# A fused attention and two-MoE kernel on one core: the rational function's square in PSUM, output sums in two banks, shifted tile addresses and a narrow block in half banks

## The chip, the core and the metric

The kernel runs on one core of one Trainium2 chip. Its engines work side by side, each through a queue of its own in a fixed order: TensorE (PE in the rows) multiplies matrices into PSUM, VectorE (DVE), ScalarE (ACT) and GpSimd (POOL) work on whole tiles, SyncE (SP) issues the transfers. PSUM has eight banks here, `ps0` to `ps7`, each 128 partitions by 512 float32; GpSimd is never given a PSUM operand in this kernel. The metric is the device time in microseconds (us), lower is better.

## What is computed

Linear attention (softmax of q over its features, of k over the sequence) feeds a gated MoE, whose output feeds a second MoE with a rational function of its hidden values. The inputs are float32; tokens are 2304, the model width 512, the hidden widths 1536 and 2048.

```python
kv  = einsum('bhsd,bhse->bhde', k_s, v)
x   = einsum('bhsd,bhde->bhse', q_s, kv)      # to (2304, 512)
x   = ((x @ w_a) * (x @ w_b)) @ w_out         # first MoE, d_ff 1536
h   = x @ w_in                                # second MoE, d_ff 2048
P   = a[0] + a[1]*h + a[2]*h**2 + a[3]*h**3
Q   = 1.0 + abs(b[0])*abs(h) + abs(b[1])*h**2
out = (P / (Q + 1e-6)) @ w_out2
```

## The kernel before

Every float32 operand of a product is split into a high and a low part, and a product is three matmuls: high by high, high by low, low by high (`mm3`, lines 444 to 447, and the same in `mult`, lines 598 to 600). The transposed activations lie in `XH` and `XL`, the running sums in `ACC`, weights and split hidden values in cuts of one long tile `wa`, everything unsplit in cuts of `fa`. Tokens are worked in four blocks of 512 and one narrow block of 256.

**First MoE.** `step1` takes one hidden block f of 128 and one token block n: products a and b (`proj`) into two banks, a copy of a by ScalarE (L473), the product by VectorE (L476), the split by ScalarE and VectorE (L479, L480), and then (`rest`) four products with `w_out` into the four banks `Y` = ps0 to ps3, which after three hidden blocks are added to `ACC` by VectorE (`add_acc`, L463). The last group of steps ends with the narrow block.

**Second MoE.** The multiplication by `w_in` goes in 16 slots of a Strassen-Winograd scheme. `operands` makes the sums and differences of the activation blocks (L520 to L527), once for blocks 0 and 1 and once for blocks 2 and 3. A slot makes seven products of six matmuls each (L598 to L600): A11 into `BA`, copied by ScalarE to `BB` (L619); S1 into `BE`, copied to s5; A12 onto `BA`; S2 onto `BB`, added with s5 by VectorE into `BC` (L624); S3 onto `BB`, added with s5 into the SBUF tile h4 (L626); S4 onto `BC`; A22 onto `BB`. The four banks are the same in every slot: BA, BE, BB, BC = 4, 5, 6, 7. The first eight slots also multiply the narrow block, into BE. Each result h goes through `value` (72 times): ScalarE makes |h| and two linear terms (L552 to L554), GpSimd w = w|h| (L559), VectorE the cubic (L558 or, for h4, GpSimd's L556; then L560), ScalarE the reciprocal square root of Q and its square u into SBUF (L562, L563), VectorE the cubic's last step times u (L564), one Newton step of the reciprocal (L566) and the product (L568). `whole` splits the value (ScalarE's L580, GpSimd's L581), and `jobs` multiplies four values by `w_out2` into the banks ps0 to ps3, four hidden blocks for each sum, then adds to `ACC` (L463) and sends the last sum out.

**What sets the order.** All work is first entered in `Plan` with an engine, an estimated duration, a rank and what it reads and writes. `Plan.run` then goes through time by these estimates: of what is ready, it takes the earliest possible start, then the lower rank. The engines' queues are the result. The estimates know nothing of VectorE and GpSimd slowing each other in `value`: only `port=True` work excludes each other there, and `value`'s VectorE work is entered without it. `LATE` is what the second half of `value` adds to its rank, `SOON` what the adds and copies inside a slot take off it.

Of the kernel before, what the change touches and what calls it, by code (L numbers as in the profile page):

```python
# [16 lines left out]
P = 128  # L17
# [97 lines left out]
def tile_kernel(ctx: ExitStack, tc: tile.TileContext, q, k, kx, v, w_a, w_b, w_out, w_in, w_out2, ca, cb, out):  # L115
# [7 lines left out]
    W = 512  # L123
# [13 lines left out]
    LATE, SOON = 1.0, -2.0  # L137
# [43 lines left out]
    fa = Area(o_x + 3 * W, F32, "fa")  # L181

# [284 lines left out]
    def step1(f, n, banks, start, stop, first, final, rank):  # L467
        t0, nb = blocks[n]
        ba, bb = banks
        proj("a", f, n, ba, rank)  # L470
        g, kg = r_g.take()
        g = g[:, :nb]
        act(nb, rank, lambda: nc.scalar.activation(g, ps[ba][:, :nb], AF.Copy), [psk(ba)], [kg])  # L473
        proj("b", f, n, bb, rank)
        p, kp = ps[bb][:, :nb], psk(bb)
        dve(nb, rank, lambda: nc.vector.tensor_tensor(out=p, in0=p, in1=g, op=ALU.mult), [kp, kg], [kp])  # L476
        hl, kh = r_hl.take()
        hh, ll = hl[:, 0, :nb], hl[:, 1, :nb]
        act(nb, rank, lambda: nc.scalar.activation(hh, p, AF.Copy), [kp], [kh])  # L479
        dve(nb, rank, lambda: nc.vector.tensor_tensor(out=ll, in0=p, in1=hh.bitcast(F32), op=ALU.subtract),  # L480
            [kp, kh], [kh])

        def rest():
            w, kw = wtile["o", f]
            for m in range(NCC):
                sl = slice(m * P, (m + 1) * P)
                pe(3, nb, rank, lambda m=m, sl=sl: mm3(ps[Y[m]][:, :nb], w[:, 0, sl], w[:, 1, sl], hh, ll, start, stop),
                   [kw, kh], [psk(Y[m])], fixed=13)
            if not stop:
                return  # L490
            for m in range(NCC):
                o = NCC * t0 + m * nb
                add_acc(o, nb, Y[m], first, rank)
                if final and nb < W:
                    a, xh, xl = ACC[:, o:o + nb], XH[:, m, t0:t0 + nb], XL[:, m, t0:t0 + nb]
                    act(nb, rank, lambda a=a, xh=xh: nc.scalar.activation(xh, a, AF.Copy),
                        [("accr", o)], xk("XH", m, t0, nb))
                    pool(nb, rank, lambda a=a, xh=xh, xl=xl: nc.gpsimd.tensor_tensor(
                        out=xl, in0=a, in1=xh.bitcast(F32), op=ALU.subtract),
                        [("accr", o)] + xk("XH", m, t0, nb), xk("XL", m, t0, nb))  # L500
        return rest

# [6 lines left out]
    def operands(pair, spots, rank, swift):  # L509
# [20 lines left out]
        for r in range(2):  # L530
# [16 lines left out]
    def value(h, kh, ring, rank, inside):  # L547

        V, A, G = nc.vector, nc.scalar, nc.gpsimd
        (u, ku), (w, kw), (z, kz) = r_t.take(), r_t.take(), ring.take()  # L550
        n = W
        act(n, rank, lambda: A.activation(u, h, AF.Abs), [kh], [ku])  # L552
        act(n, rank, lambda: A.activation(z, h, AF.Identity, scale=coef[:, 3:4], bias=coef[:, 2:3]), [kh], [kz], ptr=2)
        act(n, rank, lambda: A.activation(w, u, AF.Identity, scale=bmag[:, 1:2], bias=bmag[:, 0:1]), [ku], [kw], ptr=2)  # L554
# [7 lines left out]
        act(n, rank + LATE, lambda: A.activation(u, w, AF.Abs_reciprocal_sqrt, bias=qbias), [kw], [ku], ptr=1)  # L562
# [40 lines left out]
    BA, BE, BB, BC = 4, 5, 6, 7  # L603
    NAMES = ("A11", "S1", "A12", "S2", "S3", "S4", "A22", "A21")

    def slot(js, j, spots, extra):
# [48 lines left out]
    def jobs(n, g, base, each, banks=Y, by_m=0.0):  # L655

        t0, nb = blocks[n]
        made = {}
        for i, m in [(i, m) for i in range(G2) for m in range(nb // P)]:
            f = g * G2 + i  # L660
            w2, kw2 = w2tile[f]
            sl = slice(m * P, (m + 1) * P)
            rank = step2_rank(base, i * each + m * by_m)
            if m == 0:
                made[i] = whole(f, n, rank - 1.0)
            hl, khl = made[i]
            pe(3, W, rank, lambda m=m, sl=sl, hl=hl, w2=w2, i=i: mm3(
                ps[banks[m]], hl[:, 0, sl], hl[:, 1, sl], w2[:, 0, :], w2[:, 1, :], i == 0, i == G2 - 1),
                [kw2, khl], [psk(banks[m])], fixed=13)
        for m in range(nb // P):  # L670
            r0 = t0 + m * P
# [38 lines left out]
    for s, (n, f, a, b) in enumerate(steps):  # L710
        banks = AB if n == NB - 1 or s < NB * G1 or s % 2 == 0 else AT
# [15 lines left out]
    r_op = Ring(wa.cuts([(9 * 2 + i) * W for i in range(2)] + [i * W for i in range(6)], OP))  # L727
    r_w2 = Ring(wa.cuts([(3 + i) * 2 * W for i in range(5)], 2 * W))
    ha = pair(wa.cuts([8 * 2 * W] + [(NW + i) * 2 * W for i in range(NHL)], 2 * W))
    for i, x in enumerate((XH, XL)):  # L730
        ha.append((x[:, 2:4, 3 * W:4 * W], place(1, 3, 0)[i][1] + place(1, 3, 1)[i][1]))
# [5 lines left out]
    halves = {}  # L737
    w2tile, tile2 = {}, {}
# [82 lines left out]
```

## Time and profile before

| what | value |
|---|---|
| median of 3 runs | 968.3 us (966.86 to 969.74) |
| the profiled execution | 967.09 us, its span 965.3 us |
| TensorE busy | 919.0 us, 95% of the span |
| VectorE busy | 718.2 us, 74% |
| ScalarE busy | 554.9 us, 57% |
| GpSimd busy | 472.7 us, 49% |
| mean granted clock of TensorE | 0.988 |
| DMA queue of SyncE | 130.4 MB, 42.1% of 16 engines |

Read it with care in two places. A matmul is shown longer than the distance to the next one, since matmuls overlap, so TensorE's busy share hides part of its waiting; the distance from start to start is the better measure. And the shares are means over two halves with different work: attention and the first MoE until about 510 us, the second MoE from there. The rest of the 967.09 us beside the span lies around it.

### The profile page before, as it was taken

The page shows a single profiled execution, that of the slowest core. Times are in us where ns is not written, and L with a number is a line of the kernel's source. Part 1 is how long each engine was busy: PE and PEld are TensorE (multiplying, and loading weights), DVE is VectorE, ACT ScalarE, POOL GpSimd, SP SyncE. Part 2 cuts the span into 40 slices and gives each one's busy share as a digit, 9 for nine tenths or more (in the row PEclk, how much of TensorE's full clock was granted, in tenths as well). Part 3 has the DMA queues.
Part 4 walks back from the last instruction along what each step waited for, and adds up shares of the span by engine and source line. Part 5 has one row for each costly group of instructions (what it writes and reads, how often), then busy time and mean ns, then how long its engine had stood idle before and what let it go on. Part 6 is the DMA issues. An engine that isn't in the chain of part 4 may idle for free.

```text
span 965.3 us, 13178 instructions
## 1 busy us (share of the span) xinstructions
PE 919.0 (95%) x4576; PEld 740.9 (77%) x4576; DVE 718.2 (74%) x1035; ACT 554.9 (57%) x1046; POOL 472.7 (49%) x385
## 2 busy tenths in 40 slices
PE   8999999999999999999999879889898899999997
PEld 7677779888888888888778657778786677877775
DVE  5899641465677666766953698888997999879895
ACT  5878552453443444444421777686777667886670
POOL 4554310345423455353620447665768657574652
PEclk9999999999999999999999999999999999999999
DMA  7555510426654566545413432433324255435212
GB/s 257 189 193 152 159 29 1 130 95 222 230 174 131 176 208 213 189 133 174 152 44 96 166 89 86 139 89 106 127 80 160 77 169 179 145 97 164 69 63 87
DMA packets 60034, 131.23 MB, mean 136 GB/s; under 512 B 6464, under 2 KB 14656, under 8 KB 59968
## 3 DMA queue, kind: packets, MB, share of 16 engines
q1 hardware_dynamic: 59680, 130.39, 42.1%
q8 instruction: 36, 0.59, 0.3%
q14 instruction: 30, 0.25, 0.1%
q10 hardware_dynamic: 288, 0.00, 0.0%
HBM read 100.49 MB, written 29.88 MB: 135 GB/s over the span
## 4 chain that ended last, share of the span: by engine, by line
PE 63%; DVE 24%; issue 6%; ACT 4%; POOL 3%; DMA 1%; POOLq 0%; ACTq 0%; DVEq 0%
PE ps L445 18%; PE ps L447 17%; PE ps L446 17%; DVE fa L566 4%; DVE fa L564 4%; DVE fa L568 4%; DVE fa L560 3%; DVE ACC L463 2%; PE ps L598 2%; PE ps L600 2%; PE ps L599 2%; PE ps L426 2%; DVE fa L558 2%; DVE ACC L527 1%; PE ps L400 1%
## 5 line engine op out<-in xcount | busy, mean ns | idle before, releaser
L445 PE MATMUL ps<-XH,wa 128*128 128x512 f32 (+1 forms) x544 | 200.8, 369 | 1.1 <-ACT fa L473 1.1
L447 PE MATMUL ps<-XH,wa 128*128 128x512 f32 (+1 forms) x544 | 196.0, 360 | 0.3 <-POOL wa L288 0.3
L446 PE MATMUL ps<-XL,wa 128*128 128x512 f32 (+1 forms) x544 | 195.9, 360 | 0.0
L445 PE MATMUL ps<-wa 128*128 128x512 f32 (+1 forms) x432 | 168.2, 389 | 5.9 <-DVE ACC L463 3.8
L446 PE MATMUL ps<-wa 128*128 128x512 f32 (+1 forms) x432 | 166.2, 385 | 1.4 <-DVE wa L480 1.4
L447 PE MATMUL ps<-wa 128*128 128x512 f32 (+1 forms) x432 | 165.5, 383 | 0.1
L559 POOL TENSOR_TENSOR fa<-fa 128x512 f32<-128x512 f32 x72 | 108.0, 1511 | 38.4 <-ACT fa L554 31.9
L288 POOL TENSOR_TENSOR wa<-fa,wa 128x512 fp32r<-128x512 f32 x36 | 50.9, 1419 | 141.0 <-ACT wa L287 136.5
L445 PEld LDWEIGHTS ps<-XH,wa 128*128 128x128 f32 x544 | 102.1, 188 | 19.7 <-ACT fa L473 2.2
L447 PEld LDWEIGHTS ps<-XH,wa 128*128 128x128 f32 x544 | 102.2, 188 | 18.3 <-POOL wa L288 0.7
L598 PE MATMUL ps<-XH,wa 128*128 128x512 f32 x224 | 92.4, 413 | 24.8 <-DVE ps L624 11.2
L446 PEld LDWEIGHTS ps<-XL,wa 128*128 128x128 f32 x544 | 102.1, 188 | 16.5
L305 POOL TENSOR_TENSOR fa<-fa 128x256 fp32r<-128x256 f32 x96 | 76.9, 824 | 69.6 <-ACT fa L304 66.7
L476 DVE TENSOR_TENSOR ps<-ps,fa 128x512 f32<-128x512 f32 (+1 forms) x60 | 38.7, 645 | 95.9 <-PE ps L447 95.8
L581 POOL TENSOR_TENSOR wa<-fa,wa 128x512 fp32r<-128x512 f32 x48 | 80.1, 1680 | 53.4 <-ACT wa L580 35.0
L445 PEld LDWEIGHTS ps<-wa 128*128 128x128 f32 x432 | 82.2, 190 | 25.5 <-DVE ACC L463 5.1
L446 PEld LDWEIGHTS ps<-wa 128*128 128x128 f32 x432 | 82.3, 191 | 18.5 <-DVE wa L480 2.9
L479 ACT ACTIVATE wa<-ps 128x512 fp32r<-128x512 f32 (+1 forms) x60 | 33.2, 554 | 109.6 <-DVE ps L476 109.6
L447 PEld LDWEIGHTS ps<-wa 128*128 128x128 f32 x432 | 82.3, 191 | 16.9 <-POOL wa L581 0.9
L599 PE MATMUL ps<-XL,wa 128*128 128x512 f32 x224 | 90.5, 404 | 0.0
L600 PE MATMUL ps<-XH,wa 128*128 128x512 f32 x224 | 90.4, 403 | 0.0
L463 DVE TENSOR_TENSOR ACC<-ps,ACC 128x512 f32<-128x512 f32 (+1 forms) x114 | 71.6, 659 | 22.8 <-PE ps L447 22.7
(108 smaller groups left out, 1822.8 us busy)
## 6 DMA issues: line engine op xcount, KB each, us to landing
wa<-wi SPq DMA_DIRECT2D x120, 256.0 KB, 2.9
wi<-fa SPq DMA_DIRECT2D x64, 256.0 KB, 3.7
wa<-wo SPq DMA_DIRECT2D x32, 512.0 KB, 3.4
fa<-in_moe_w_out SPq DMA_DIRECT2D x28, 512.0 KB, 4.3
fa<-in_moe_w_in SPq DMA_DIRECT2D x16, 512.0 KB, 3.8
wo<-fa SPq DMA_DIRECT2D x32, 256.0 KB, 4.3
fa<-in_moe_w_a SPq DMA_DIRECT2D x12, 512.0 KB, 4.5
fa<-in_moe_w_b SPq DMA_DIRECT2D x12, 512.0 KB, 3.6
```

What stands on the lines that cost most here:

```text
L288: pool(W, rank, lambda: nc.gpsimd.tensor_tensor(out=t[:, 1, :], in0=hf, in1=t[:, 0, :].bitcast(F32), op=ALU.subtract), [kr, kw], [kw])
L305: pool(HALF, rank, lambda: nc.gpsimd.tensor_tensor(out=lo, in0=src, in1=hi.bitcast(F32), op=ALU.subtract), [ksrc, kt], [kt])
L445: nc.tensor.matmul(o, lh, rh, start=start, stop=False)
L446: nc.tensor.matmul(o, lh, rl, start=False, stop=False)
L447: nc.tensor.matmul(o, ll, rh, start=False, stop=stop)
L463: dve(n, rank, lambda: nc.vector.tensor_tensor(out=a, in0=ps[bank][:, :n], in1=a, op=ALU.add), [psk(bank), ("accr", o)], [("accr", o)])
L476: dve(nb, rank, lambda: nc.vector.tensor_tensor(out=p, in0=p, in1=g, op=ALU.mult), [kp, kg], [kp])
L559: pool(n, rank, lambda: G.tensor_tensor(out=w, in0=w, in1=u, op=ALU.mult), [ku, kw], [kw])
L581: pool(W, rank, lambda: nc.gpsimd.tensor_tensor(out=hl[:, 1, :], in0=z, in1=hl[:, 0, :].bitcast(F32), op=ALU.subtract), [kz, kh], [kh])
L598: T.matmul(ps[bank], wh, xh, start=first, stop=False, skip_group_check=True)
L599: T.matmul(ps[bank], wh, xl, start=False, stop=False, skip_group_check=True)
L600: T.matmul(ps[bank], wl, xh, start=False, stop=last, skip_group_check=True)
```

## The change

Five things change; the arithmetic of the result does not, apart from the order of some subtractions in `operands`.

- `value` takes a PSUM bank for every h. The square of the reciprocal square root goes back into that bank (h) instead of an SBUF tile (u), so the three closing VectorE operations each read h from PSUM, and the Newton step writes it. S3's add goes into the bank of S1 instead of the SBUF tile h4, and its first multiplication from GpSimd to VectorE. `LATE` is 0.25 instead of 1.0.
- The four fixed product banks become two rings of three: 5, 3, 4 for BA, BE and the narrow products, 6, 7, 2 for BB and BC. One matmul at the start of the second MoE writes bank 2 once. The output sums have ps0 and ps1 only: `jobs` runs through the four hidden blocks for two token chunks, then for the next two.
- `small`, `mx` and `ks` (320 bytes of each partition, every tile rounded up to 32) are allocated behind `wa` and `fa` instead of in front of them, so `wa` and `fa` begin 320 bytes lower.
- The last group of the narrow block in the first MoE leaves `step1` for `last_narrow`: products a and b share one bank in halves, the output sums two banks in halves, and the ranks are `LAST` = 60.3 and up, so its work falls among the first slots.
- Tiles for operands, `w_out2` and split values take other places in `wa`, and four operand tiles lie in XH and XL where two split values lay.

```diff
-    LATE, SOON = 1.0, -2.0
+    LAST = 60.3
+    LATE, SOON = 0.25, -2.0
...
+
+    small = tiles(2, [P, 4 * C5], F32, "small")
+    mxs = tiles(2, [P, 1], F32, "mx")
+    kss = tiles(2, [P, 1], F32, "ks")
...
+    def last_narrow(fs, ranks):
+        n = NB - 1
+        t0, nb = blocks[n]
+        bank, (y0, y1) = 4, (0, 1)
+        left, right = ps[bank][:, :nb], ps[bank][:, nb:2 * nb]
+        hs = []
+        for f, rank in zip(fs, ranks):
+            for kind, o, ko in (("a", left, ("half", 0)), ("b", right, ("half", 1))):
+                w, kw = wtile[kind, f]
...
+                if kind == "a":
+                    g, kg = r_g.take()
+                    g = g[:, :nb]
+                    act(nb, rank, lambda g=g: nc.scalar.activation(g, left, AF.Copy), [("half", 0)], [kg])
+            dve(nb, rank, lambda g=g: nc.vector.tensor_tensor(out=right, in0=right, in1=g, op=ALU.mult),
+                [("half", 1), kg], [("half", 1)])
...
+        for m in range(NCC):
+            sl = slice(m * P, (m + 1) * P)
+            bank = (y0, y1)[m // 2]
+            y, ky = ps[bank][:, m % 2 * nb:(m % 2 + 1) * nb], ("halfy", m)
...
-        if inside:
-            pool(n, rank, lambda: G.tensor_tensor(out=z, in0=z, in1=h, op=ALU.mult), [kz, kh], [kz])
-        else:
-            dve(n, rank, lambda: V.tensor_tensor(out=z, in0=z, in1=h, op=ALU.mult), [kz, kh], [kz])
         pool(n, rank, lambda: G.tensor_tensor(out=w, in0=w, in1=u, op=ALU.mult), [ku, kw], [kw])
+        dve(n, rank, lambda: V.tensor_tensor(out=z, in0=z, in1=h, op=ALU.mult), [kz, kh], [kz])
...
-        act(n, rank + LATE, lambda: A.activation(u, u, AF.Square), [ku], [ku])
-        dve(n, rank + LATE, lambda: V.scalar_tensor_tensor(
-            out=z, in0=z, scalar=coef[:, 0:1], in1=u, op0=ALU.add, op1=ALU.mult), [kz, ku], [kz], ptr=1)
-        dve(n, rank + LATE, lambda: V.scalar_tensor_tensor(
-            out=u, in0=w, scalar=qbias, in1=u, op0=ALU.add, op1=ALU.mult), [kw, ku], [ku], ptr=1)
-        dve(n, rank + LATE, lambda: V.scalar_tensor_tensor(
-            out=z, in0=u, scalar=2.0, in1=z, op0=ALU.subtract, op1=ALU.mult, reverse0=True), [ku, kz], [kz])
+        rank += LATE
+        act(n, rank, lambda: A.activation(u, w, AF.Abs_reciprocal_sqrt, bias=qbias), [kw], [ku], ptr=1)
+        act(n, rank, lambda: A.activation(h, u, AF.Square), [ku], [kh])
+        dve(n, rank, lambda: V.scalar_tensor_tensor(
+            out=z, in0=z, scalar=coef[:, 0:1], in1=h, op0=ALU.add, op1=ALU.mult), [kz, kh], [kz], ptr=1)
+        dve(n, rank, lambda: V.scalar_tensor_tensor(
+            out=h, in0=w, scalar=qbias, in1=h, op0=ALU.add, op1=ALU.mult), [kw, kh], [kh], ptr=1)
+        dve(n, rank, lambda: V.scalar_tensor_tensor(
+            out=z, in0=h, scalar=2.0, in1=z, op0=ALU.subtract, op1=ALU.mult, reverse0=True), [kh, kz], [kz])
...
-    BA, BE, BB, BC = 4, 5, 6, 7
...
+        ba, be, bb, bc = r_free.take(), r_free.take(), r_seed.take(), r_seed.take()
...
-        dve(W, R(0.2) + SOON, lambda: V.tensor_tensor(out=h4, in0=ps[BB], in1=s5, op=ALU.add), [psk(BB), k5], [k4])
+        dve(W, R(0.2) + SOON, lambda: V.tensor_tensor(out=ps[be], in0=ps[bb], in1=s5, op=ALU.add), [psk(bb), k5], [psk(be)])
...
-    def jobs(n, g, base, each, banks=Y, by_m=0.0):
+    def jobs(n, g, base, each, banks=None, by_m=0.5):
...
+        banks = banks or Y2 * 2
...
+                rank = step2_rank(base, i * each + m // 2 * by_m + m * 0.01)
...
+    spare = [(x[:, 2 + r, 3 * W:4 * W], place(1, 3, r)[i][1]) for i, x in enumerate((XH, XL)) for r in range(2)]
+    r_op = Ring(wa.cuts([(6 * 2 + i) * W for i in range(2)], OP) + spare + wa.cuts([(7 * 2 + i) * W for i in range(2)], OP))
+    r_w2 = Ring(wt(9, 0, 1, 3, 4))
+    ha = pair(wt(8, NW, NW + 1, NW + 2, 2, 5))
...
+    r_free, r_seed = Ring((5, 3, 4)), Ring((6, 7, 2))
+    Y2 = (0, 1)
```

The order of the queues up to about 480 us is the same in both. Two places of the second MoE show what moved. The number after an underscore is a tile's running number; in the changed kernel `ps`, `wa` and `fa` have lower ones. L603, L605 and L607 are there what L564, L566 and L568 are before, L597 and L598 what L558 and L560 are, L663 and L465 what L624 and L463 are.

VectorE's queue ahead of the add that makes `BC` in the seventh slot, in the kernel before:

```order
L568 SCALAR_TENSOR_TENSOR fa_89<-fa_89 128x512
L566 SCALAR_TENSOR_TENSOR fa_89<-fa_89,qbias_66 128x512
L564 SCALAR_TENSOR_TENSOR fa_89<-fa_89,coef_64 128x512
L568 SCALAR_TENSOR_TENSOR fa_89<-fa_89 128x512
L566 SCALAR_TENSOR_TENSOR fa_89<-fa_89,qbias_66 128x512
L564 SCALAR_TENSOR_TENSOR fa_89<-fa_89,coef_64 128x512
L568 SCALAR_TENSOR_TENSOR fa_89<-fa_89 128x512
L566 SCALAR_TENSOR_TENSOR fa_89<-fa_89,qbias_66 128x512
L568 SCALAR_TENSOR_TENSOR fa_89<-fa_89 128x512
L624 TENSOR_TENSOR ps7_87<-ps6_86,fa_89 128x512
```

VectorE's queue ahead of the same slot's add in the changed kernel:

```order
L603 SCALAR_TENSOR_TENSOR fa_83<-fa_83,coef_64,ps7_81 128x512
L465 TENSOR_TENSOR ACC_73<-ps0_74,ACC_73 128x512
L605 SCALAR_TENSOR_TENSOR ps7_81<-fa_83,qbias_66,ps7_81 128x512
L465 TENSOR_TENSOR ACC_73<-ps1_75,ACC_73 128x512
L607 SCALAR_TENSOR_TENSOR fa_83<-ps7_81,fa_83 128x512
L597 TENSOR_TENSOR fa_83<-fa_83,ps4_78 128x512
L597 TENSOR_TENSOR fa_83<-fa_83,ps5_79 128x512
L598 SCALAR_TENSOR_TENSOR fa_83<-fa_83,coef_64,ps4_78 128x512
L598 SCALAR_TENSOR_TENSOR fa_83<-fa_83,coef_64,ps5_79 128x512
L663 TENSOR_TENSOR ps7_81<-ps6_80,fa_83 128x512
```

Before, nine closing operations with SBUF operands alone stand in a row ahead of the add; after, closing operations, output adds and opening operations alternate, and each has a PSUM operand.

TensorE's queue from the last matmul of one output sum in ps0 to the first of the next, in the second half of the slots, in the kernel before:

```order
L447 MATMUL ps0_80<-wa_88 128x512
L445 MATMUL ps1_81<-wa_88 128x512
L446 MATMUL ps1_81<-wa_88 128x512
L447 MATMUL ps1_81<-wa_88 128x512
L445 MATMUL ps2_82<-wa_88 128x512
L446 MATMUL ps2_82<-wa_88 128x512
L447 MATMUL ps2_82<-wa_88 128x512
L445 MATMUL ps3_83<-wa_88 128x512
L446 MATMUL ps3_83<-wa_88 128x512
L447 MATMUL ps3_83<-wa_88 128x512
L445 MATMUL ps0_80<-wa_88 128x512
```

The same from one sum in ps0 to the next in the changed kernel, in the same half:

```order
L449 MATMUL ps0_74<-wa_82 128x512
L447 MATMUL ps1_75<-wa_82 128x512
L448 MATMUL ps1_75<-wa_82 128x512
L449 MATMUL ps1_75<-wa_82 128x512
L637 MATMUL ps3_77<-XH_71,wa_82 128x512
L638 MATMUL ps3_77<-XL_72,wa_82 128x512
L639 MATMUL ps3_77<-XH_71,wa_82 128x512
L447 MATMUL ps0_74<-wa_82 128x512
```

Before, the sums of three other banks stand between, nine matmuls; after, the sum in ps1 and half a product of a slot, six.

## Rows read from the trace of the kernel before

**Rows 1.** Busy time in two stretches: engines (instructions), granted clock, DMA share, GB/s.

```profile
180.00:480.00 300.00, 300.00 (x1403) 246.97 (x1402) 206.73 (x347) 130.09 (x257) 136.78 (x151) 1.00 0.54 175
505.00:961.00 456.00, 420.56 (x1887) 337.87 (x1886) 385.65 (x460) 305.48 (x512) 266.56 (x175) 0.97 0.36 115
```

**Rows 2.** Matmul groups by line and form, 505 to 962 us: busy us, mean ns, idle before.

```profile
L598 PE MATMUL ps<-XH,wa 128*128 128x512 f32 x224 | 92.4, 413 | 24.8 <-DVE ps L624 11.2 <-ACT ps L619 6.7 <-DVE fa L626 3.7
...
L445 PE MATMUL ps<-wa 128*128 128x512 f32 x200 | 80.7, 403 | 5.9 <-DVE ACC L463 3.8 <-ACT fa L562 2.1
...
L445 PE MATMUL ps<-XH,wa 128*128 128x256 f32 x88 | 24.8, 282 | 1.1 <-ACT fa L473 1.1
...
L445 PE MATMUL ps<-wa,XH 128*128 128x512 f32 x48 | 19.5, 406 | 1.4 <-ACT fa L553 0.6 <-DVE ACC L463 0.5 <-ACT XH L580 0.2
```

**Rows 3.** TensorE in order of time, first matmuls of unbroken streams: start us, length us.

```profile
302.32 0.39 PE L445 MATMUL ps<-wa 128*128 128x512 f32 x1
...
305.06 0.39 PE L445 MATMUL ps<-XH,wa 128*128 128x512 f32 x1
...
310.66 0.39 PE L445 MATMUL ps<-wa 128*128 128x512 f32 x1
...
622.38 0.28 PE L445 MATMUL ps<-XH,wa 128*128 128x256 f32 x1
...
625.21 0.39 PE L445 MATMUL ps<-wa 128*128 128x512 f32 x1
...
634.17 0.40 PE L445 MATMUL ps<-wa,XL 128*128 128x512 f32 x1
...
636.25 0.39 PE L598 MATMUL ps<-XH,wa 128*128 128x512 f32 x1
```

**Rows 4.** Who waited for whom, 500 to 965 us: us in total, times, longest.

```profile
DVE fa L564 <- ACT fa L563: 11.4, 10, 2.0
PE ps L598 <- DVE ps L624: 11.2, 7, 2.9
...
PE ps L598 <- ACT ps L619: 6.7, 2, 3.6
...
PE ps L445 <- DVE ACC L463: 4.3, 2, 3.8
```

**Rows 5.** Busy time around one longer wait, columns as in rows 1.

```profile
740.00:745.00 5.00, 1.78 (x8) 1.13 (x6) 4.96 (x6) 5.00 (x10) 5.00 (x4) 0.96 0.76 240
745.00:750.00 5.00, 4.43 (x10) 3.47 (x11) 5.00 (x9) 1.44 (x3) 2.79 (x3) 0.50 0.01 4
```

**Rows 6.** VectorE's scalar_tensor_tensor groups of `value` by form, columns as in rows 2.

```profile
L568 DVE SCALAR_TENSOR_TENSOR fa<-fa 128x512 f32<-128x512 f32 x72 | 78.2, 1093 | 0.7
L564 DVE SCALAR_TENSOR_TENSOR fa<-fa,coef 128x512 f32<-128x512 f32 x72 | 75.5, 1058 | 11.6 <-ACT fa L563 11.4
L566 DVE SCALAR_TENSOR_TENSOR fa<-fa,qbias 128x512 f32<-128x512 f32 x72 | 72.5, 1016 | 1.7
...
L560 DVE SCALAR_TENSOR_TENSOR fa<-fa,coef,ps 128x512 f32<-128x512 f32 x56 | 41.2, 743 | 1.0
...
L560 DVE SCALAR_TENSOR_TENSOR fa<-fa,coef 128x512 f32<-128x512 f32 x16 | 25.5, 1592 | 6.6 <-POOL fa L556 6.6
```

**Rows 7.** One line's instructions: shortest, median and longest in ns.

```profile
L564 DVE SCALAR_TENSOR_TENSOR fa<-fa,coef x72: 739/751/1885, 541.1 to 945.2; 128x512 f32<-128x512 f32 x72
```

**Rows 8.** Three engines in order of time around one wait, in brackets idle us before.

```profile
691.87 5.14 POOL L581 TENSOR_TENSOR wa<-fa,wa 128x512 fp32r<-128x512 f32 x3
...
699.15 0.69 DVE L624 TENSOR_TENSOR ps<-ps,fa 128x512 f32<-128x512 f32 x1
...
699.89 0.50 PE L598 MATMUL ps<-XH,wa 128*128 128x512 f32 x1 [2.93 <-DVE ps L624]
```

**Rows 9.** The chain that ended last, in order of time: start us, us, what.

```profile
689.48 0.66 DVE fa L564
...
692.45 1.70 DVE fa L564
```

More of the change, by code (lines that the diff above doesn't have):

```diff
@@ L493, in rest @@
                 add_acc(o, nb, Y[m], first, rank)
[L494 to L500, printed above, removed]
@@ L545, in step2_rank, with value @@
         return n1 + SLOT * (js + x)
-    def value(h, kh, ring, rank, inside):
+    def value(bank, ring, rank):
         V, A, G = nc.vector, nc.scalar, nc.gpsimd
+        h, kh = ps[bank], psk(bank)
         (u, ku), (w, kw), (z, kz) = r_t.take(), r_t.take(), ring.take()
@@ L624, in slot @@
-        dve(W, R(0.15) + SOON, lambda: V.tensor_tensor(out=ps[BC], in0=ps[BB], in1=s5, op=ALU.add), [psk(BB), k5], [psk(BC)])
-        mult(BB, ops["S3"], t3, False, True, R(0.2))
-        dve(W, R(0.2) + SOON, lambda: V.tensor_tensor(out=h4, in0=ps[BB], in1=s5, op=ALU.add), [psk(BB), k5], [k4])
-        mult(BC, ops["S4"], e22, False, True, R(0.25))
-        mult(BB, ops["A22"], t4, False, True, R(0.3))
+        (s5, k5) = r_s.take()
+        ba, be, bb, bc = r_free.take(), r_free.take(), r_seed.take(), r_seed.take()
@@ new lines, in slot @@
+        mult(ba, ops["A11"], e11, True, False, R(0.0))
+        act(W, R(0.0) + SOON, lambda: A.activation(ps[bb], ps[ba], AF.Copy), [psk(ba)], [psk(bb)])
+        mult(be, ops["S1"], t1, True, True, R(0.05))
+        act(W, R(0.05) + SOON, lambda: A.activation(s5, ps[be], AF.Copy), [psk(be)], [k5])
+        mult(ba, ops["A12"], e21, False, True, R(0.1))
+        mult(bb, ops["S2"], t2, False, True, R(0.15))
+        dve(W, R(0.15) + SOON, lambda: V.tensor_tensor(out=ps[bc], in0=ps[bb], in1=s5, op=ALU.add), [psk(bb), k5], [psk(bc)])
@@ L636, in slot @@
         t0, nb = blocks[-1]
+        bx = r_free.take()
         for i, (lo, hi) in enumerate((("A11", "A12"), ("A21", "A22"))):
@@ L653, in second @@
             w2tile[f] = (t.rearrange(two, a=2), k)
-    def jobs(n, g, base, each, banks=Y, by_m=0.0):
+    def jobs(n, g, base, each, banks=None, by_m=0.5):
         t0, nb = blocks[n]
+        banks = banks or Y2 * 2
         made = {}
[L659 to L669, printed above, removed]
-        for m in range(nb // P):
+        for m in range(nb // P):
+            for i in range(G2):
+                f = g * G2 + i
+                w2, kw2 = w2tile[f]
+                rank = step2_rank(base, i * each + m // 2 * by_m + m * 0.01)
+                if m == 0:
+                    made[i] = whole(f, n, rank - 1.0)
+                hl, khl = made[i]
+                sl = slice(m * P, (m + 1) * P)
+                pe(3, W, rank, lambda m=m, sl=sl, hl=hl, w2=w2, i=i: mm3(
+                    ps[banks[m]], hl[:, 0, sl], hl[:, 1, sl], w2[:, 0, :], w2[:, 1, :], i == 0, i == G2 - 1),
+                    [kw2, khl], [psk(banks[m])], fixed=13)
             r0 = t0 + m * P
@@ L710, in tile_kernel @@
     for s, (n, f, a, b) in enumerate(steps):
+        if n == NB - 1 and b == NF1:
+            if f == a:
+                pend()
+                last_narrow(range(a, b), [LAST + 0.1 * i for i in range(b - a)])
+                pend = lambda: None
+            put_weights(s - 1)
+            while s >= S0 and spills and len(spills) * (S1 - S0) > (S1 - s) * 3 * NP2:
+                spills.pop(0)(s + 1.0)
+            continue
         banks = AB if n == NB - 1 or s < NB * G1 or s % 2 == 0 else AT
@@ L724, in tile_kernel @@
     assert not spills
[L727 to L731, printed above, removed]
+    wt = lambda *ids: [wa.cut(i * 2 * W, 2 * W) for i in ids]
+    spare = [(x[:, 2 + r, 3 * W:4 * W], place(1, 3, r)[i][1]) for i, x in enumerate((XH, XL)) for r in range(2)]
+    r_op = Ring(wa.cuts([(6 * 2 + i) * W for i in range(2)], OP) + spare + wa.cuts([(7 * 2 + i) * W for i in range(2)], OP))
+    r_w2 = Ring(wt(9, 0, 1, 3, 4))
+    ha = pair(wt(8, NW, NW + 1, NW + 2, 2, 5))
     r_o = Ring(ha)
@@ L748, in tile_kernel @@
         slot(js, js % NP2, spots[js // NP2], extra)
+        if js == 0:
+            pe(1, W, step2_rank(0, 0.2), lambda: nc.tensor.matmul(ps[2], minus, XH[:, 0, 0:W], start=True, stop=True),
+               xk("XH", 0, 0, W) + [psk(2)], [psk(2)], fixed=13)
         if js == NP2 - 1:
```

66 lines of the change are left out of this document (41 added, 25 removed).

## The prediction

> **What bounds the kernel now.** I read the stages first. From 180 to 480 us TensorE is busy for all 300 us, and over the second MoE (505 to 961 us) for 420.6 of 456 us at a mean granted clock of 0.97, with VectorE at 385.7 and ScalarE at 305.5 us [rows 1]. A busy TensorE is not yet a full one, so I count the work: matmuls of each form [rows 2] times the pace of an unbroken stream, start to start [rows 3]. With a 512-column moving operand out of XH or XL and weights in wa it is (310.66 - 305.06)/24 = 0.2333 us; with both in wa (305.06 - 302.32)/12 = 0.2283; moving from wa with weights in XL (636.25 - 634.17)/9 = 0.231; with 256 columns (625.21 - 622.38)/24 = 0.118. The stage holds 672 products of the transformed multiply (224 on each of three lines, one shown), 600 output products out of wa (200 on each of three lines) and 288 with hl in XH or XL (48 on each of six lines), 264 narrow ones (88 times 3), and 63 more that end the first MoE, about 11 us: 156.8 + 137.0 + 66.5 + 31.2 + 11 = 402 us. The last matmul ends at about 961.4, 456 us after 505. So **54 us of the stage are not work**, and that is what any reordering can win there; the stage from 180 to 480 has none.
>
> Where the 54 go: the waits of TensorE name DVE's L624 (11.2 us, 7 times), ACT's L619 (6.7, twice), DVE's L463 (4.3, twice) [rows 4], then smaller ones. [...] The mean of 0.97 puts 3% of 456 us, some 12 us, on the clock; the rest is waiting.
>
> Why VectorE is late there is the key reading. Its scalar_tensor_tensor forms are alike in work, but those with a PSUM operand mean 743 ns (L560, 56 of them) while those with SBUF operands alone mean 1,058, 1,016 and 1,093 (L564, L566, L568) and 1,592 (L560 on h4) [rows 6]. L564 alone goes from 739 to 1,885 ns [rows 7]. One place shows it: GpSimd runs from 691.87 for 5.14 us, the add L624 starts only at 699.15, and TensorE, which waits for that add, loses 2.93 us [rows 8]; in the chain of waits L564 takes 0.66 us to the next start before GpSimd's stretch and 1.70 inside it [rows 9]. Two operations that both read SBUF get in each other's way; one with a PSUM operand does not.
>
> **The change part by part.**
> Square into PSUM. It keeps the count of VectorE's operations (L556 moves there from GpSimd), but L564, L566, L568 and the h4 forms of L560 now have a PSUM operand. The trace has no such form of L566 and L568; the nearest rows are L560's 743 ns and, without a pointer scalar, L624's 690 [rows 6, 8]. VectorE saves 75.5 - 72 x 0.743 = 22.0 us, 72.5 - 53.5 = 19.0, 78.2 - 72 x 0.69 = 28.5 and 25.5 - 16 x 0.743 = 13.6, and pays 16 x 0.743 = 11.9 for L556: **71 us less**, 385.7 to about 314, that is from 85% of 456 us to 78% of 402. From the other side, if PSUM forms cost 0.1 us more than those rows, 23 us of it go back and the share is 84%. GpSimd, 266.6 us now [rows 1], loses 16 multiplications and bounds nothing. The subtractions of the second operand pair (L527) keep two SBUF operands; collisions stay there.
> What that is worth on TensorE: in the example five operations of 1.7 us stand ahead of the add; at 0.66 us each [rows 9] they end 5 us sooner, and the 2.93 us wait has no cause left. The order ahead of the same add (section on the change) also changes: before, nine closing operations that all read SBUF alone; after, two output adds and seven operations that all have a PSUM operand.
>
> [...]
>
> Two output banks, six product banks. The products rotate over six banks, so a slot's first product no longer waits for the last reader of the slot before; that is the cause behind the 3.6 us wait on ACT's L619. The output sums shrink from four banks to two, so TensorE restarts a bank sooner after its last product. The order shows it (section on the change): nine matmuls (2.1 us) of cover become six (1.4 us). Of 66 such restarts after, 28 have six and 4 have three; the others nine or more. Before, 60 of 64 had nine, and they cost 4.3 us in two waits [rows 4]. What a restart needs with VectorE free is the matmul's own drain (0.39 long, 0.23 to the next start: 0.16), an add of 0.69 and 0.05 to the start [rows 3, 8], 0.9 us; so six leave 0.5 us, less than one VectorE operation. I give each of the 32 tight ones 0.2 us, 6.4 us.
>
> Narrow block in half banks. The same matmuls, but they need one bank and two half-used ones instead of six, and stand between the first slots' products. Nothing is saved on them; they are cover where TensorE now waits (3.6 us at most) [rows 4]. Its product a waits for ScalarE's copy of the left half, its product b for three operations on the right half, at an estimated 0.45 us each (a 512-column add takes 0.69) some 1.6 us with the handovers; behind them on TensorE stand the first slots. Between them stand the other product's twelve narrow matmuls (1.4 us) and mostly six or twelve wide ones, so I take 0 to 2 us, and 0. One extra matmul costs 0.2 us. Weight and operand tiles change places; the longest waits of TensorE name no DMA [rows 4].
>
> What stays: 6.4 us of restarts, 6 for the 48 handoffs inside the slots (17.9 us now [rows 4], a third of it), 2 at the end where the last value is awaited, 3 for a slow stretch or two: 17.4, taken as **18 of the 54 us**. The bounds are 8 (free restarts, half the rest) and 30 (0.5 us for each tight restart, and what L527's collisions keep of the 3.8 us wait on L463 [rows 4]).
>
> Equal remainders. small, mx and ks take 320 bytes per partition between ACC and wa, so wa starts 64 bytes off XH modulo 128; moved behind fa, all start alike. The pace is 0.2283 where both operands have the same remainder, 0.2333 and 0.231 where not [rows 3]. If that is the cause, 1,152 wide projections of the first MoE and 672 products of the second gain 0.005 us each, 9 us, all on TensorE's path. If only the region matters, nothing; if the moving operand's remainder alone does, the 1,440 matmuls out of wa lose 0.005 each, 7 us more. Both mixed rows lie above the equal one, so I take the 9.
>
> Sum: 967.1 (the profiled execution) - 54 + 18 - 9 = 922; the median of the runs is 1.2 above that execution: **923 us**. Differences under 0.3% (3 us) count as no change.
>
> **The rivals.**
> Addresses do nothing or harm (0.20): 932, or up to 939.
> The waits are of the order, not of the collisions (0.12): half of the 54 us stay; 967.1 - 27 - 9 + 1.2 = 932 with the addresses, 941 without, up to 946 with more slow clock. For it: ACT's load hardly falls, and VectorE waited 11.4 us for L563 [rows 4]. Against: the slow operations stand right ahead of the late adds [rows 8].
> Slower (0.07): VectorE's queue stops for ACT in front of an output add. LATE falls from 1.0 to 0.25, so the closing operations stand close behind ACT's Square; if each of 66 adds sits behind such a stop of 2.0 us (the longest wait of L564 on L563) [rows 4], TensorE loses 2.0 less a cover of 0.5 to 1.2, about 1 us, each: 923 + 66 = 989. It decides from 0.7 us for each restart (45 us won over 66).
> It does nothing (0.03): PSUM forms as slow as the SBUF ones; 965 to 970.
> Better (0.08): 8 us stay, 912.
>
> **How the numbers follow.** Forecast 923 with 0.50; the rest as above. The range 912 to 946 takes in the bounds of what stays (8 to 30) and most of the address rival, and leaves out the slower case and the worst of the order case. Faster 0.90, within 0.3% 0.03, slower 0.07.
>
> **What would show it.** L603, L605 and L607 at 0.69 to 0.76 us with no maximum above 0.9; VectorE's busy time from the stage's start near 314 us; the multiply's pace at 0.228; no wait of TensorE above 2.5 us after 510. I am wrong if the PSUM forms run above 0.85 us, or if waits on the output add (L465) sum to over 20 us.

## The result, and the profile after

The changed kernel takes **920.85 us** (median of 4 runs, 919.76 to 924.02) against 968.22: a ratio of 0.9516, with a 95% interval of 0.9489 to 0.9543. The forecast was 923, its range 912 to 946. The profiled execution took 919.76 us, its span is 917.7.

Where the 47.6 us between the two spans went can be read from the start of the same matmul in both traces. The queues agree up to about 480 us, and the matmul that starts at 518.27 us before (the seventh of the last twelve wide ones of the first MoE) starts at 512.49 after: 5.8 us, won where TensorE hardly waits (from 180 us to there 1.9 us in three waits before, 2.9 in three after). The last product starts at 961.07 before and at 913.43 after, so the second MoE gives the other 42 us.

Stages of the changed kernel, columns as in [rows 1]; the second line is the stage shifted by what was won ahead of it:

```profile
180.00:480.00 300.00, 297.56 (x1411) 249.62 (x1410) 211.60 (x354) 132.96 (x263) 136.43 (x151) 1.00 0.54 175
...
498.90:913.40 414.50, 403.94 (x1889) 334.83 (x1888) 315.69 (x476) 304.95 (x512) 203.80 (x159) 0.99 0.40 126
```

VectorE is busy for 315.7 us in place of 385.7, GpSimd for 203.8 in place of 266.6; TensorE's granted clock goes from 0.97 to 0.99. VectorE's groups in the second MoE answer to [rows 6], the source line under them to [rows 7] (shortest, median and longest in ns):

```profile
L598 DVE SCALAR_TENSOR_TENSOR fa<-fa,coef,ps 128x512 f32<-128x512 f32 x72 | 53.2, 741 | 0.8
L605 DVE SCALAR_TENSOR_TENSOR ps<-fa,qbias,ps 128x512 f32<-128x512 f32 x72 | 53.2, 747 | 0.0
L603 DVE SCALAR_TENSOR_TENSOR fa<-fa,coef,ps 128x512 f32<-128x512 f32 x72 | 52.9, 743 | 28.7 <-ACT ps L602 28.4
...
L607 DVE SCALAR_TENSOR_TENSOR fa<-ps,fa 128x512 f32<-128x512 f32 x72 | 48.6, 683 | 0.6
```

```profile
L603 DVE SCALAR_TENSOR_TENSOR fa<-fa,coef,ps x72: 729/743/750, 525.1 to 895.7; 128x512 f32<-128x512 f32 x72
```

No operation of L603 is longer than 750 ns; its counterpart L564 went up to 1,885 [rows 7]. The waits of the changed kernel, 480 to 918 us, answer to [rows 4] (VectorE's largest first, then TensorE's):

```profile
DVE fa L603 <- ACT ps L602: 28.4, 26, 3.6
...
PE ps L449 <- POOL wa L620: 3.9, 3, 2.6
...
PE ps L637 <- DVE ps L663: 1.3, 1, 1.3
...
PEld ps L447 <- DVE ACC L465: 1.3, 4, 0.5
```

VectorE now waits more for ScalarE than before (28.4 us, not 11.4), and TensorE hardly feels it: L663, which stands for the 11.2 us of L624, costs 1.3, and the output sums cost four short delays of a weight load (PEld) and no wait of a matmul. The pace of unbroken streams answers to [rows 3]:

```profile
299.62 0.39 PE L447 MATMUL ps<-wa 128*128 128x512 f32 x1
...
301.66 0.39 PE L447 MATMUL ps<-XH,wa 128*128 128x512 f32 x1
...
307.10 0.39 PE L447 MATMUL ps<-wa 128*128 128x512 f32 x1
```

(307.10 - 301.66)/24 = 0.2267 us where XH or XL moves, (301.66 - 299.62)/9 = 0.2267 where both lie in wa. Before it was 0.2333 and 0.2283.

### The profile page after: what moved, and what is told of

It is laid out like the page before. It is cut to its first block, busy times and chain, and to the rows that moved or that the text cites. A ratio compares the mean times of both kernels' runs of the same rounds, so it can differ in the third digit from the quotient of the medians.

```text
span 917.7 us, 13161 instructions
## 1 busy us (share of the span) xinstructions
PE 893.9 (97%) x4577; PEld 737.3 (80%) x4577; DVE 647.5 (71%) x1051; ACT 554.1 (60%) x1046; POOL 408.9 (45%) x369
## 4 chain that ended last, share of the span: by engine, by line
PE 89%; DVE 5%; ACT 3%; POOL 2%; issue 1%; DMA 1%; ACTq 0%; POOLq 0%; DVEq 0%
PE ps L447 23%; PE ps L449 23%; PE ps L448 23%; PE ps L637 5%; PE ps L639 5%; PE ps L638 5%; PE ps L428 2%; PE ps L402 1%; PE ps L418 1%; DVE ACC L567 1%; DMA coef<-in_moe_b 1%; DVE ACC L465 1%; PE ps L369 1%; DVE fa L280 0%; POOL fa L319 0%
## 5 line engine op out<-in xcount | busy, mean ns | idle before, releaser
L447 PE MATMUL ps<-wa 128*128 128x512 f32 (+1 forms) x528 | 203.9, 386 | 3.4 <-ACT wa L481 1.4
L449 PE MATMUL ps<-wa 128*128 128x512 f32 (+1 forms) x528 | 201.7, 382 | 3.9 <-POOL wa L620 3.9
L448 PE MATMUL ps<-wa 128*128 128x512 f32 (+1 forms) x528 | 201.6, 382 | 1.0 <-DVE wa L482 1.0
L447 PE MATMUL ps<-XH,wa 128*128 128x512 f32 (+1 forms) x528 | 195.5, 370 | 2.7 <-DVE ps L519 1.1
L449 PE MATMUL ps<-XH,wa 128*128 128x512 f32 (+1 forms) x528 | 190.5, 361 | 0.2 <-POOL wa L290 0.2
L448 PE MATMUL ps<-XL,wa 128*128 128x512 f32 (+1 forms) x528 | 190.4, 361 | 0.0
L596 POOL TENSOR_TENSOR fa<-fa 128x512 f32<-128x512 f32 x72 | 93.8, 1307 | 128.2 <-ACT fa L594 117.4
L620 POOL TENSOR_TENSOR wa<-fa,wa 128x512 fp32r<-128x512 f32 x72 | 93.2, 1311 | 61.7 <-ACT wa L619 48.1
L447 PEld LDWEIGHTS ps<-wa 128*128 128x128 f32 x528 | 99.6, 189 | 25.1 <-ACT wa L619 2.0
L449 PEld LDWEIGHTS ps<-wa 128*128 128x128 f32 x528 | 99.7, 189 | 24.4 <-POOL wa L620 5.5
L447 PEld LDWEIGHTS ps<-XH,wa 128*128 128x128 f32 x528 | 99.7, 189 | 20.2 <-ACT wa L523 1.4
L448 PEld LDWEIGHTS ps<-wa 128*128 128x128 f32 x528 | 99.8, 189 | 20.0 <-DVE wa L482 1.8
L290 POOL TENSOR_TENSOR wa<-fa,wa 128x512 fp32r<-128x512 f32 x36 | 50.3, 1403 | 139.5 <-ACT wa L289 135.2
L449 PEld LDWEIGHTS ps<-XH,wa 128*128 128x128 f32 x528 | 99.6, 189 | 15.9 <-POOL wa L290 0.7
L465 DVE TENSOR_TENSOR ACC<-ps,ACC 128x512 f32<-128x512 f32 (+1 forms) x110 | 72.2, 670 | 36.1 <-PE ps L449 35.9
L603 DVE SCALAR_TENSOR_TENSOR fa<-fa,coef,ps 128x512 f32<-128x512 f32 x72 | 52.9, 743 | 28.7 <-ACT ps L602 28.4
L279 ACT ACTIVATE fa<-fa 128x512 f32<-128x512 f32 x68 | 45.7, 680 | 30.9 <-DVE fa L277 30.3
L597 DVE TENSOR_TENSOR fa<-fa,ps 128x512 f32<-128x512 f32 x72 | 49.1, 683 | 21.3 <-ACT fa L595 21.1
```

The source lines that it names most:

```text
L290: pool(W, rank, lambda: nc.gpsimd.tensor_tensor(out=t[:, 1, :], in0=hf, in1=t[:, 0, :].bitcast(F32), op=ALU.subtract), [kr, kw], [kw])
L447: nc.tensor.matmul(o, lh, rh, start=start, stop=False)
L448: nc.tensor.matmul(o, lh, rl, start=False, stop=False)
L449: nc.tensor.matmul(o, ll, rh, start=False, stop=stop)
L465: dve(n, rank, lambda: nc.vector.tensor_tensor(out=a, in0=ps[bank][:, :n], in1=a, op=ALU.add), [psk(bank), ("accr", o)], [("accr", o)])
L603: dve(n, rank, lambda: V.scalar_tensor_tensor(out=z, in0=z, scalar=coef[:, 0:1], in1=h, op0=ALU.add, op1=ALU.mult), [kz, kh], [kz], ptr=1)
```

## The experiments

Medians in us; every ratio is to the kernel before, run on the same chip beside it.

| kernel | us | ratio, 95% interval |
|---|---|---|
| changed | 920.85 | 0.9516 (0.9489 to 0.9543) |
| tiles back in front | 929.05 | 0.9601 (0.9578 to 0.9623) |
| before, tiles moved alone | 962.29 | 0.9937 (0.9914 to 0.9959) |
| control for the square | 923.38 | 0.9539 (0.9514 to 0.9563) |
| square in SBUF | 973.91 | 1.0071 (1.0045 to 1.0096) |
| before, square in PSUM alone | 974.81 | 1.0066 (1.0051 to 1.0082) |
| the same, LATE 0.25 | 956.52 | 0.9878 (0.9864 to 0.9893) |
| four output, four product banks | 943.14 | 0.9742 (0.9725 to 0.9758) |
| LATE = 1.0 | 927.18 | 0.9576 (0.9562 to 0.9591) |
| narrow block as before | 924.98 | 0.9562 (0.9546 to 0.9578) |
| other remainders | 927.17 (one run) | |
| LAST = 61.0 | 930.46 | 0.9613 (0.9597 to 0.9629) |
| seven splits on GpSimd | 924.71 | 0.9554 (0.9540 to 0.9570) |

**Do VectorE and GpSimd get in each other's way?** Two kernels with the same order of every queue differ only in where the square and the Newton step lie. The control is the changed kernel, with u kept in use as long as the other needs it (shown for the first of four steps):

```diff
-        act(n, rank, lambda: A.activation(h, u, AF.Square), [ku], [kh])
+        act(n, rank, lambda: A.activation(h, u, AF.Square), [ku], [ku, kh])
```

> Control for the next run: the changed kernel, square in PSUM, but the plan is told that the tile u of the reciprocal square root stays in use until the last step, as it has to where the square lies in u. That shifts the order somewhat. Both theories expect little: 921 to 926 us.

The other has u for h in that line and in L603, L605 and L607 (one of them shown):

```diff
-            out=h, in0=w, scalar=qbias, in1=h, op0=ALU.add, op1=ALU.mult), [kw, ku, kh], [ku, kh], ptr=1)
+            out=u, in0=w, scalar=qbias, in1=u, op0=ALU.add, op1=ALU.mult), [kw, ku, kh], [ku, kh], ptr=1)
```

> As the control, with the same order of every queue and the same holding of banks, but the square and the Newton step in the SBUF tile u, so that L603, L605 and L607 have SBUF operands alone. If VectorE and GpSimd getting in each other's way is what cost the waits: the three lines at 0.95 to 1.1 us mean with longest ones near 1.9, VectorE's busy time up by 50 to 80 us, TensorE's waits back, 940 us (930 to 955). Rival, that order and banks won the time: within 4 us of the control.

The control took 923.38 us, the SBUF form 973.91: **50.5 us** from the place of one tile, more than either theory gave. Its VectorE groups and its waits of TensorE, second MoE:

```profile
L605 DVE SCALAR_TENSOR_TENSOR fa<-fa,qbias 128x512 f32<-128x512 f32 x72 | 81.1, 1134 | 1.8
L603 DVE SCALAR_TENSOR_TENSOR fa<-fa,coef 128x512 f32<-128x512 f32 x72 | 74.7, 1046 | 16.0 <-ACT fa L602 15.3
L607 DVE SCALAR_TENSOR_TENSOR fa<-fa 128x512 f32<-128x512 f32 x72 | 69.7, 976 | 0.6
```

```profile
PE ps L637 <- DVE ps L663: 18.7, 10, 3.8
PE ps L447 <- DVE ACC L465: 10.5, 8, 3.4
```

The busy time from 505 us to the end, first the control's, then this kernel's:

```profile
505.00:970.00 465.00, 400.14 (x1872) 330.70 (x1870) 312.85 (x475) 303.31 (x511) 203.95 (x159) 0.99 0.35 114
```

```profile
505.00:970.00 465.00, 418.62 (x1870) 336.50 (x1868) 384.69 (x475) 303.54 (x510) 226.21 (x159) 0.97 0.36 113
```

VectorE works 72 us longer, GpSimd 22, and TensorE's granted clock is 0.97 in place of 0.99. One line's shortest, median and longest, first the control's, then the SBUF form's:

```profile
L603 DVE SCALAR_TENSOR_TENSOR fa<-fa,coef,ps x72: 732/742/749, 527.3 to 899.1; 128x512 f32<-128x512 f32 x72
```

```profile
L603 DVE SCALAR_TENSOR_TENSOR fa<-fa,coef x72: 734/752/1815, 526.8 to 948.7; 128x512 f32<-128x512 f32 x72
```

The slow ones are those that meet GpSimd: of the 216 operations of L603, L605 and L607 in the SBUF form, 95 have no GpSimd operation beside them, and none of these takes over 753 ns; of the other 121, 90 take over 900. In the control 143 have one beside them, and none takes over 752. Undisturbed, both forms take about the same time: the shortest of L603, L605 and L607 are 729, 741 and 671 ns in the changed kernel, 734, 735 and 674 in the SBUF form. What L603's SBUF form adds, up to 1.08 us, stays below one whole GpSimd operation (1.27 us at the shortest, L596). What makes the two engines hold each other up is not shown.

The rival (order and banks won the time) falls: with the order and banks of the changed kernel and the square in SBUF the time is above that of the kernel before. And here, with slow operations, the two output banks are as tight as feared: 10.5 us on L465.

**Is the square in PSUM enough alone?** The kernel before, with the square in the product's bank for the 56 values that have one:

```diff
-        act(n, rank + LATE, lambda: A.activation(u, u, AF.Square), [ku], [ku])
+        q, kq = (u, ku) if inside else (h, kh)
+        act(n, rank + LATE, lambda: A.activation(q, u, AF.Square), [ku], [kq])
```

and q for u in the three steps behind it. The plan is made anew by it, so the order of the queues is not quite that of before.

> The kernel before with the square and the Newton step in the product's bank for the 56 values that have one (not for those of h4), and nothing else: four fixed product banks, four output banks, LATE = 1.0. If the collisions are most of the loss and the banks come free in time: L564, L566 and L568 at 0.69 to 0.76 us in their PSUM form, 935 to 950 us. Rival, that four banks can't be held so long: waits of L598 on L619 or L568 take the gain back, 955 to 985 us.

974.81 us, 0.7% slower than before, though L565, its last cubic step, runs at 739 ns. The rival was right:

```profile
L565 DVE SCALAR_TENSOR_TENSOR fa<-fa,coef,ps 128x512 f32<-128x512 f32 x56 | 40.8, 739 | 1.6 <-ACT ps L564 0.4
```

```profile
PE ps L445 <- ACT wa L581: 18.7, 5, 7.6
PE ps L599 <- DVE fa L569: 11.5, 3, 7.9
```

L569 is the last step of `value` there: a product's bank comes free only after it, up to 7.9 us late, and the output products wait for values that are late in turn. So LATE = 0.25 was tried with it:

> The kernel before with the square in PSUM as in the run of that name, and LATE = 0.25 as well: still four fixed product banks and four output banks. If that run lost because the closing operations came late and so held the banks: most of its two kinds of waits (output products on the split, a product's bank on the last step) go, 940 to 950 us. If four fixed banks are too few whatever LATE is: 960 us or more.

956.52 us, between the two expectations: the waits on L569 are gone, those on the split shrink from 18.7 to 11.0 us, and those on the copy to `BB` (L620) grow from 2.5 to 8.8.

```profile
PE ps L445 <- ACT wa L581: 11.0, 3, 6.5
PE ps L599 <- ACT ps L620: 8.8, 4, 5.7
```

**Are the six product banks needed?** The changed kernel with the banks of before (`jobs` goes through the four output banks as before too, not shown):

```diff
-    r_free, r_seed = Ring((5, 3, 4)), Ring((6, 7, 2))
-    Y2 = (0, 1)
+    r_free, r_seed = Ring((5, 4)), Ring((6, 7))
+    Y2 = (0, 1, 2, 3)
```

> The changed kernel with the banks of before: output sums over four banks (ps0 to ps3), products over two rings of two (5, 4 and 6, 7). The square stays in PSUM, so a product's bank is held until the last step of its value. If six product banks are needed for that: TensorE waits for L658, L663 or the first product of a slot, 5 to 30 us in sum, 935 us (925 to 955). Rival, that the short restarts of two output banks cost as much as six product banks bring: 917 to 923 us.

943.14 us, 22 more. Two groups of waits of TensorE, for a product's bank, make 20.5 us of it (the copy L658 itself waits 7.5 us for L607, the last reader of such a bank):

```profile
PE ps L637 <- ACT ps L658: 12.7, 5, 4.9
PE ps L637 <- DVE fa L607: 7.8, 5, 2.9
```

**LATE alone**, 1.0 in the changed kernel:

> The changed kernel with LATE = 1.0, so that the closing operations stand later in VectorE's queue, as in the kernel before. With the square in PSUM a bank is held longer by it: if that is what LATE is for, products wait for banks, 923 to 935 us, with waits of L637 on L658 or on L607. Rival, that only the collisions mattered: 919 to 923 us.

927.18 us, 6.3 more, on the wait that was named:

```profile
PE ps L637 <- DVE fa L607: 5.8, 2, 3.1
```

**The narrow block** back in `step1`, in full banks:

> The changed kernel with the last group of the narrow block done as before (full banks, four output banks, at the end of the first MoE). The prediction put this part at 0 to 2 us and took 0. If the work standing among the first slots is cover: 2 to 6 us slower, 923 to 927 us, with the loss between 480 and 570 us. Rival, nothing: 919 to 923 us.

924.98 us, 4.1 more, not far above the 3 us that the prediction calls no change (runs of 923.90 to 926.92 against 919.76 to 924.02). The size was as expected. The largest wait is at 553.65 us:

```profile
553.65 0.79 PE L644 MATMUL ps<-XH,XL 128*128 128x512 f32 x1 [5.72 <-DVE ps L670]
```

L670 is the add that makes `BC`. It stood in VectorE's queue behind operations of `value` that ran from 549.09 us on without a pause: the first slots' values come in a crowd where no narrow work stands between them.

**The addresses.** First undone in the changed kernel, then done alone in the kernel before; both leave every queue's order as it was.

```diff
+    small = tiles(2, [P, 4 * C5], F32, "small")
+    mxs = tiles(2, [P, 1], F32, "mx")
+    kss = tiles(2, [P, 1], F32, "ks")
     ps = [psum.tile([P, W], F32, name=f"ps{i}") for i in range(8)]
```

> The changed kernel with small, mx and ks back in front of wa, so that wa starts 64 bytes off XH and XL again; every queue has the same order as in the changed kernel. If the equal address remainders are the cause of the faster matmuls: 0.2332 us from start to start where XH or XL moves and wa holds the weights, still 0.227 to 0.229 where both lie in wa (or both in XH and XL), and 11 us more over all, about 932 us (929 to 934). Rival, that the pace came with another order or with fewer waits: 0.227 everywhere and 921 us.

929.05 us, 8.2 more. The pace is that of the kernel before again, (310.09 - 304.49)/24 = 0.2333:

```profile
304.49 0.39 PE L447 MATMUL ps<-XH,wa 128*128 128x512 f32 x1
...
310.09 0.39 PE L447 MATMUL ps<-wa 128*128 128x512 f32 x1
```

> The kernel before with small, mx and ks moved behind fa and nothing else; every queue has the same order as before. If the remainders are the cause: 0.227 for every 512-column pair, 6 us less up to 505 us where TensorE never waits, and 0 to 6 us less in the second MoE, where it waits for VectorE and what it saves can turn into longer waits: 957 us (955 to 962). Rival, that addresses do nothing by themselves: 968 us.

962.29 us, 6.3 less, just outside what was expected. The matmul of 518.27 us starts 5.8 us earlier, the last one 5.6: the second MoE kept nothing of its faster matmuls, since TensorE waited longer for VectorE. The wait on L624 grew from the 11.2 us of [rows 4]:

```profile
PE ps L598 <- DVE ps L624: 14.0, 8, 3.2
```

Then other remainders: 96 bytes ahead of XL and 32 ahead of wa.

> The changed kernel with 96 bytes in front of XL and 32 in front of wa, so that modulo 256 XH starts at 0, XL at 96 and wa at 128. If the remainder modulo 128 decides, as the equal starts suggest: 0.227 to 0.229 us where XH moves and wa holds the weights, 0.230 to 0.234 where XL moves. If it is modulo 256: 0.230 or more for both. If only multiples of 32 matter: 0.227 for all.

```profile
303.73 0.40 PE L449 MATMUL ps<-XH,wa 128*128 128x512 f32 x1
...
309.28 0.39 PE L449 MATMUL ps<-wa 128*128 128x512 f32 x1
```

(309.28 - 303.73)/24 = 0.2313 over matmuls that move XH and XL in turn. Apart, with the start of every matmul set against the addresses of its operands, they are 0.2315 (876 with XH, 128 bytes off wa) and 0.2304 (487 with XL, 224 off). Both are slow, so equal remainders modulo 128 don't suffice. Modulo 256 fits these two, but no rule on one product's two operands fits all. Some products have both in XH, or both in XL, so their remainders are equal in every kernel; yet in unbroken streams they take 0.2316 and 0.2314 us here, 0.2269 and 0.2276 in the changed kernel. That addresses alone change the pace is shown; which relation of them does is open.

**Two tries at a faster kernel**, `LAST = 61.0`, and `operands(1, ...)` with 2 in place of 3 as its last argument.

> A try at a faster kernel: the changed kernel with LAST = 61.0, so that the narrow block's last group spreads over more of the first slots' work. TensorE waits there for L518, L519, L523 and L538 about 3 us now. If more cover takes them: 917 to 920 us. Rival, that the later sums delay the first slots' values: 921 to 925 us.

> A try at a faster kernel: the changed kernel with ten of the twenty splits of the second operand pair on GpSimd in place of thirteen. The longest wait left is 2.6 us for a GpSimd split (L620) that stands behind four of these. If that is all: 916 to 919 us. Rival, that three more subtractions with two SBUF operands on VectorE collide with GpSimd and give it back: 921 to 924 us.

930.46 and 924.71 us: neither beats the changed kernel, and the first is slower than both of its expectations. Its longest waits are now 4.6 us on L518 and 4.0 on L663. The second moves three splits, but the counts in its expectation are wrong: the second operand pair has 14 splits, ten of them on GpSimd in the changed kernel and seven here. Its longest wait is now for a subtraction of VectorE with two SBUF operands:

```profile
PE ps L638 <- DVE XL L564: 2.7, 1, 2.7
```

## Why the prediction was right, and where it wasn't

**The bound (54 us that are not work): right.** Counted the same way, with the 0.2272 us that a 512-column matmul takes in the mean of the stage's unbroken streams, 18.9 us of the changed stage are not work, 35.6 less than before. With the addresses, 6.2 us up to the stage and 5.8 of faster matmuls in it, that makes the 47.6. Undoing the addresses costs 8.2 us, not these 12, so part of the 12 is not shown to be theirs.

**Collisions as the reason: right, and larger than thought.** VectorE's saving was taken as 71 us; it is 70 between the kernels and 72 between control and SBUF form. What it was worth on TensorE was read as most of 36 us. With the new banks it is 50.5: TensorE waits 18.7 us for L663 and 10.5 for L465 in the SBUF form, against 11.2 and 4.3 for their counterparts before. That the two output banks and the short LATE leave a slow VectorE less room than the old order did is likely, but neither was undone in the SBUF form. With a PSUM operand L603 is not slower: its median is 742 ns with one (control) and 752 without (SBUF form).

**What stays (18 us): right as a sum by luck, wrong in its terms.** The 6.4 us for tight restarts aren't there: four delays of a weight load, 1.3 us. The step that failed is the cover against an estimated 0.9 us; an add that VectorE takes at once (0.69 us, the median of L465) is done within six matmuls (1.36 us at 0.227 each), and no matmul waited for L465. The handoffs inside the slots were priced at 6 and cost 2.0 (L663 1.3, L658 0.7). In their place stand two things that I had at nothing: the waits for a split (L620 3.9, L619 1.2) and those of the narrow block, 3.0 (L519, L523, L518, L538). So 9.1 us too much stood against 8.1 that were missing. The clock was put at 3 for a slow stretch or two; no run shows that figure. In the changed kernel one stretch, 725 to 735 us, ran at 0.67 and 0.65, and the stage's mean of 0.99 makes an estimated 4 us (1% of 414.5); about 3.5 of the 18.9 stand in no row named here. The largest wait is a queue with a collision at its end. GpSimd, ScalarE, VectorE and TensorE of the changed kernel, in order of time:

```profile
720.95 3.79 POOL L562 TENSOR_TENSOR XL<-ACC,XH 128x512 fp32r<-128x512 f32 x3 [0.26 <-ACT XH L560]
...
722.44 0.61 ACT L619 ACTIVATE wa<-fa 128x512 fp32r<-128x512 f32 x1
...
723.61 1.68 DVE L564 TENSOR_TENSOR XL<-ACC,XH 128x512 fp32r<-128x512 f32 x1
...
724.69 1.72 POOL L620 TENSOR_TENSOR wa<-fa,wa 128x512 fp32r<-128x512 f32 x1
...
726.47 0.61 PE L449 MATMUL ps<-wa 128*128 128x512 f32 x1 [2.63 <-POOL wa L620]
```

ScalarE's half of the split is done at 723.05, but GpSimd is on three operand splits until 724.7; that is 1.6 us of the wait. The subtraction then reads SBUF alone and takes 1.68 us beside GpSimd, whose split takes 1.72 instead of its mean 1.31: an estimated 0.4 us (1.72 - 1.31) is the collision. Of the signs named ahead, the one that allowed no wait above 2.5 us failed here, by 0.13. L607 runs at a mean of 683 ns, just below its band; the others held.

**The narrow block at 0: wrong by 4 us.** I asked only how late its own chain would be, not that its matmuls spread the first slots' values.

**The banks: the step was incomplete.** Six product banks were credited with the 3.6 us wait on L619. What I left out is that the square in PSUM holds a product's bank to the last step of its value. Without the six banks 22 us of the gain are lost; the square alone, in the kernel before, loses instead of winning (974.81). LATE, which stood only in the slower rival, is a gain of 6.3 us for the same reason. The forecast was not hurt, since the change brings the parts together.

**Equal remainders: right in size, wrong in the rule.** 9 us were taken, 8.2 measured by undoing them. In the kernel before the same edit gives 6.3, for the reason that the waits take the rest. The words "modulo 128" don't hold (0.2315 us at 128 bytes off), and modulo 256 doesn't explain every stream either (0.2316 and 0.2314 with equal remainders); in the change the difference is 0 modulo 256, and every pair of operands has a mean between 0.2269 and 0.2276.

**The slower rival** needed VectorE to stop for ScalarE ahead of output adds. It does stop, 26 times and 28.4 us, but with 315.7 busy of 414.5 us it has the time, and no matmul waits for L465. Where VectorE is 72 us busier, that wait is there, 10.5 us. How it would go without GpSimd's work was not tried.

## What to carry over

Before an engine's load is counted, look at whether its operations of equal work have equal times: here one line had a long tail (0.74 to 1.89 us), in the SBUF form every closing operation over 753 ns had a GpSimd operation beside it, and moving one operand to PSUM was worth 50.5 us with the same order of every queue. But such a move holds the new place longer: here the square in PSUM loses 0.7% without the banks and the earlier closing steps that it needs, and the whole change, which has them, wins 4.8%. In the kernel before, the faster matmuls alone were worth 5.8 us where TensorE hardly waited, and nothing in the second MoE, where its wait for VectorE's L624 grew from 11.2 to 14.0 us.

## What was not expected of the hardware

- The pace of a 512-column matmul changes with the start addresses of its two operands. In the changed kernel, where these are equal modulo 256 bytes for every pair, the means by pair are 0.2269 to 0.2276 us from 180 us on; before, 0.2334 where the moving operand starts 192 bytes past the weights (from XH or XL, weights in wa) and 0.231 at 64 (the other way round); with the other remainders 0.2315 at 128 and 0.2304 at 224. Equal remainders alone were not enough: 0.2283 in the stream of [rows 3] where both lie in wa, 0.2316 and 0.2314 with the other remainders where both lie in XH or both in XL.
- Getting in each other's way is mutual, which I had not counted on: GpSimd is busy for 226.21 us in the SBUF form and for 203.95 in the control. Its split into wa takes 1,311 ns in the mean after and 1,680 before, though its operands are of the same kind; before (L581) stands first:

```profile
L581 POOL TENSOR_TENSOR wa<-fa,wa 128x512 fp32r<-128x512 f32 x48 | 80.1, 1680 | 53.4 <-ACT wa L580 35.0 <-issue 13.3 <-PE ps L447 3.2
```


```profile
L620 POOL TENSOR_TENSOR wa<-fa,wa 128x512 fp32r<-128x512 f32 x72 | 93.2, 1311 | 61.7 <-ACT wa L619 48.1
```
